# Query and key kept once as high and low parts, and four experts' scores made as pairs of 64-row products

## The chip, the cores and the metric

The kernel runs on one core of one Trainium2 chip. The metric is device microseconds of one execution; less is better. The profile names the engines PE (TensorE, the matrix unit, with PEld for its weight loads), DVE (VectorE), ACT (ScalarE), POOL (GpSimd) and SP (SyncE, which issues most DMAs).

## The reference, cut to what matters

Three blocks run one behind the other on 4 sequences (batches) of 576 rows: an attention with banded and strided masks, a gated feed-forward block, and a mixture of four dense attention experts. The change is in the last:

```
for e in range(E):                       # E = 4, Hd = 64, x is 4 x 576 x 512
    q = x @ wq[e];  k = x @ wk[e];  v = x @ wv[e]
    scores = scale * (q @ k.transpose(0, 2, 1))
    scores = np.where(causal, -1000000000.0, scores)
    scores = scores - scores.max(-1, keepdims=True)
    a = np.exp(scores)
    a /= a.sum(-1, keepdims=True) + 1e-09
    ye = a @ v @ wo[e]
    out += (weight of expert e in its row's top 2, else 0) * ye
```

The weights `wq` and `wk` are scaled by 200, so the scores are large and have to be made with nearly full fp32 precision.

## The kernel before, in words

**Units and order.** The work is cut into some 900 named units. `PLAN` lists them by rank; a name begins with its batch: `0k01` is a key projection of batch 0, `0s20` the scores of its query tile 2 for expert 0, `0p20` the transposes of those, `0a10` a value product, `0o12` an output projection. While the kernel is built, a `Recorder` collects every engine instruction of every unit with an estimated price (`price`), and `order` (line 384) gives them out one at a time: of the operations that could start about now on an engine it takes the one of least rank, where a change of TensorE's tile shape (`change`, with the constants `INTO` and `FROM`) sets an operation back by `stay` ranks. The order of each engine's instructions is then fixed as given out. All instructions are issued from one helper line, so every row of the profile says L484; tiles are told apart by name.

**Stages.** From the start to about 327 us the masked attention and the feed-forward block of all four batches run. Then a new SBUF pool (`p3`) is opened, and the dense experts of the four batches run until the end, with the projections of a later batch between the attention of an earlier one.

**Precision.** Products of the later blocks use the type fp32r, in which one operand is a rounded value. A value is split in a high part (rounded copy) and a low part (value minus copy); a product is then high x high, high x low and low x high (`split`, line 564). In the first block, and for batch 0 partly in the second, plain fp32 products are used; one such product in the program is two instructions in the trace.

**Queries and keys of the experts (`proj_units`, line 1356; `qkp`, line 1401).** A projection makes two experts' queries (or keys) at once, 64 rows each, in one PSUM bank. Queries: the bank is copied, both halves, for each of the two experts into a tile `Q` of 128 rows by 4 x 576; then, of each expert's columns, the 64 rows that aren't its own are overwritten with its low part. So a column block of `Q` holds high and low part of one expert one above the other. Keys: the bank is copied for both experts into `KH`, the low part into `KL`, and four DMAs from the POOL queue copy each expert's own rows into the other 64 rows. So each of `KH` and `KL` holds one expert's key part twice, one above the other.

**Scores (`tile_units`, `sc`, line 1505).** For a query tile t of 128 rows and an expert, two 128-row products with (t+1) x 128 columns are summed in one PSUM bank: `Q` with `KH`, and `Q` with `KL`. VectorE adds the mask, scales and takes the row extreme (tile `pe`), ScalarE makes the exponentials with their sum. The last 64 query rows of a sequence (`tail_units`, line 1550) are done for two experts side by side with a padded query tile `QT`, in four products of 288 columns per part.

**Banks.** Eight PSUM banks: three for scores (`ps_sc`), three for projections, value products and outputs (`ps_mm`), two for transposes (`ps_tr`).

Of the kernel before, what the change touches and what calls it, by code (L numbers as in the profile page):

```python
# [27 lines left out]
1S3 0P15 0Am5 0Am1 0W16 0Am6 1S4 0W18 0Am7 0P7 0P6 0L17 0W17 0P18 0Zg1 0Av4 2L1 0Av0 0P19 2L2 0Zg0 0Zk0 0P16 0Zg3 0P5 0P17
1V4 0P9 0Av6 0Zk2 1S6 0Av2 0Zk3 0P4 0Zk1 0Zm0 0Zg2 0sig 0P10 0Zm2 1T6 0Zm1 2z 1V6 0Zm3 0Av7 2L3 0Av3 1S8 1T8 1Ar0 0Av1 0P11
0P8 0Zm6 wl2 1Ar1 0Zm4 1V8 1Ak0 1Ak1 3z 0P3 1Ar2 3L0 0Zv4 0Zm7 0P1 0Zm5 0Zv0 1Ar3 1Ak3 0P2 0Zv1 0P0 0Av5 0x0 1Ag1 wl0 ws00  # L30
2S1 2S0 1Ak2 0Zv2 0Zv3 1Zr0 1Am4 1Zr1 1Zr2 2V1 1Zr3 1Ag0 1Am0 1Am1 1Zk0 2S4 2S3 1Ag2 0Zv6 2V4 2Ar0 2S6 2T6 1Am5 1Ag3 1Am2
1Am3 1Am6 1Am7 1Zg0 ws01 1Av4 1Zg1 wl1 0Zv5 1Zg2 2Ak0 1Zk2 3L1 2Ar1 2V6 2Ar2 0Zv7 1Zk1 1Av2 1Zg3 1Av3 3L2 1Zk3 1Av6 1Zm0 1Zm1
1Zm4 1Av0 1Av1 1Zm5 1Zm6 1Zm2 2S8 1Zm3 1Zv6 1Zm7 1Zv7 2T8 1Zv0 1Av7 2V8 2Ar3 2Ak3 2Ag1 3S1 2Ag3 2Ag0 3S0 3V1 2Ak2 ws10 3S3
3S4 2Ak1 2Am0 ws20 2Zr0 2Zr2 1Zv2 1Zv3 3V4 2Zk0 1Zv1 2Am2 1Av5 3S6 2Am3 1Zv4 1Zv5 ws21 2Zr1 2Ag2 2Am4 2Am1 2Am5 3L3 2Am6 2Am7
2Av6 2Zr3 2Zg2 3T6 3S8 2Av4 2Zg0 3V6 2Zg1 2Zg3 3T8 3V8 3Ar0 2Zk1 2Av5 2Zk2 2Zk3 3Ak0 2Zm2 2Zm6 2Zm3 2Av2 2Av0 2Av3 2Av1 2Zm0
2Zm1 2Zm4 3Ar1 2Zm5 2Zv2 3Ar2 3Ar3 0x1 3Ag0 2Zm7 2Zv3 3Zr0 2Zv6 3Ak2 3Ag2 3Ak1 2Zv4 1x0 2Av7 2Zv5 3Ag3 3Ak3 3Am4 0v0 3Am0
ws31 2Zv0 2Zv1 3Am1 3Ag1 3Zr2 3Zr1 3Am2 3Zk0 3Am5 3Am3 3Am6 3Am7 3Zr3 3Zg2 3Zg0 3Zg1 2u 2Zv7 3Zg3 3Av4 3Zk3 3Zk2 3Zk1 3Zm0
3Zm1 3Av6 3Av0 3Zm6 3Av2 3Zm2 3Zm3 3Zm4 3Zm5 3Zm7 3Zv4 3Zv6 3Zv0 3Av1 3Zv2 ws11 0k01 0k00 0q10 0k10 0q01 0k11 1u 0v4 0q00 0v1
0v2 0v3 0u 0g 3Av3 0q11 3Zv1 0s20 0s30 0s33 0s23 1k00 0t 1v1 1x1 3Zv5 0s21 1k01 0s31 0s22 0s00 1q00 0s32 0m2 0p22 0s01 0p20
0m3 0p31 1k10 3Zv3 0s02 1k11 0p33 0s40 0s03 0p30 0s10 3Zv7 0s12 1v0 0p23 0p32 1q11 1q01 2x0 0m0 0p21 0s41 0m4 3Av7 0p40 1q10  # L40
0p41 1s30 0s11 1v3 1v2 0s13 1n 1g 0m1 0p11 0p13 0p10 0p02 0p12 1s32 0p00 2q01 0a10 1s20 1s22 1s21 0a11 1s31 1s33 1m3 1p31
0p03 1p30 1s00 1s02 1s03 2x1 2q10 2k00 1s01 1s23 1m2 1s10 1s11 1s13 0p01 2k01 1s12 2k10 0o12 2q11 2t 1p21 0a00 0a01 0o01 0o11
2k11 2v3 1t 1s40 1m1 1p10 1s41 1p12 3Av5 3x1 2s30 2s33 1p32 2s32 2s20 2s21 1m0 1p02 1p22 2s23 2s22 2v2 2v4 3n 2s31 1p23 2q00
1p00 2v1 1p20 3k11 0o10 1p33 1m4 1p41 2s00 2s10 1p13 0o02 2s01 2s02 0o03 0o13 2v0 3k10 0o00 2g 2s03 2m0 1p40 3q10 1p01 1p11
# [1715 lines left out]
```

## Time and profile before

| what | us |
|---|---|
| time, median of 3 runs (lowest, highest) | 507.53 (507.33, 509.13) |
| the profiled execution's own time | 507.9 |
| its span (first to last instruction) | 506.1 |
| PE busy, weight loads busy | 495.5 (98%), 466.3 (92%) |
| DVE busy, ACT busy, POOL busy | 362.0, 288.9, 38.8 |

The span is what the trace shows; the rest of an execution's time, 1.8 us here, lies around it. Busy times of one engine are the union of its instructions. Matmuls overlap each other in the trace, so the pace of PE is read from the distance between the starts of neighbouring instructions, not from their durations.

### The profile page before, as it was taken

To read this page: it belongs to the slowest core of one execution; us is meant where nothing else is said; L and a number is where in the kernel's file an instruction comes from. 1 tells how busy PE (TensorE), PEld (TensorE's weight loads), DVE (VectorE), ACT (ScalarE), POOL (GpSimd) and SP (SyncE) were. 2 spreads that over 40 slices of the span, in tenths; PEclk is the share of its full clock that TensorE was granted. 3 is DMA by queue.
4 is the path that set the end of the run, shared out by engine and by line. 5 is a ranking of instruction groups with operands and counts; after the bars stand their busy time and mean duration, and the time that the engine had idled before them with its cause. 6 is when DMAs were issued, how large, how long until landed. Compare 5 with 4: busy or idle time off the path is not lost.

```text
span 506.1 us, 13080 instructions
## 1 busy us (share of the span) xinstructions
PE 495.5 (98%) x5080; PEld 466.3 (92%) x5080; DVE 362.0 (72%) x1230; ACT 288.9 (57%) x813; POOL 38.8 (8%) x95
## 2 busy tenths in 40 slices
PE   8799999999999999998999999999999999999997
PEld 7567799999999999998999999999998999899886
DVE  5899999894869563867574604258999887897941
ACT  6899976555548443535432533145676666367663
POOL 0000000000000000000000000053500411400000
PEclk9799999999999999999999999999999999999999
DMA  7998332332233122012321001164511422310122
GB/s 262 322 397 249 116 119 69 88 97 76 85 87 101 33 82 83 23 44 68 94 89 65 2 16 37 43 163 100 121 53 54 104 68 75 69 38 25 49 95 95
DMA packets 42008, 48.82 MB, mean 96 GB/s; under 512 B 14122, under 2 KB 36442, under 8 KB 41946
## 3 DMA queue, kind: packets, MB, share of 16 engines
q1 hardware_dynamic: 36826, 43.26, 27.2%
q0 software_dynamic: 5120, 4.72, 4.7%
q8 instruction: 40, 0.66, 0.6%
q14 instruction: 22, 0.18, 0.1%
HBM read 33.67 MB, written 9.44 MB: 85 GB/s over the span
## 4 chain that ended last, share of the span: by engine, by line
PE 92%; DMA 5%; DVE 2%; SPq 1%; issue 0%; ACT 0%; ACTq 0%
PE pk L484 19%; PE pv L484 19%; PE pr L484 11%; PE s L484 6%; PE pvv L484 5%; PE pw L484 5%; PE pq_True L484 5%; PE pq_False L484 5%; PE py L484 4%; PE pt L484 4%; DMA qkv<-in_strd_dram 2%; PE ss L484 2%; PE pol L484 2%; PE sl L484 2%; PE pos L484 2%; DMA qkv<-in_loc_dram 1%
## 5 line engine op out<-in xcount | busy, mean ns | idle before, releaser
L484 PE MATMUL pv<-kk,wvh 128*128 128x320 f32 (+1 forms) x512 | 103.8, 296 | 0.1
L484 PEld LDWEIGHTS pv<-kk,wvh 128*128 128x128 f32 x512 | 81.7, 188 | 0.8 <-DVE kk L484 0.3
L484 PE MATMUL pk<-xh,wkh 128*128 128x256 f32 (+1 forms) x224 | 65.7, 293 | 1.3 <-DVE sg L484 1.3
L484 PE MATMUL pk<-xl,wkh 128*128 128x256 f32 (+1 forms) x224 | 65.3, 291 | 0.0
L484 ACT ACTIVATE rf<-pk 128x320 f32<-128x320 f32 (+1 forms) x64 | 26.2, 409 | 48.5 <-PE pk L484 44.0
L484 ACT ACTIVATE pe<-pe,nm 128x384 f32<-128x384 f32 (+4 forms) x72 | 41.6, 580 | 10.2 <-DVE pe L484 6.7
L484 PEld LDWEIGHTS pk<-xh,wkh 128*128 128x128 f32 x224 | 42.0, 188 | 1.6 <-DVE sg L484 1.5
L484 PEld LDWEIGHTS pk<-xl,wkh 128*128 128x128 f32 x224 | 42.0, 188 | 0.0
L484 DVE TENSOR_TENSOR sg<-pv,sg 128x320 f32<-128x320 f32 (+1 forms) x32 | 14.4, 452 | 37.5 <-PE pv L484 37.2
L484 DVE CUSTOM_DVE_ANT_0 pe<-s,mcau 128x384 f32<-128x384 f32 (+4 forms) x72 | 32.8, 482 | 5.5 <-PE pt L484 3.1
L484 DVE TENSOR_TENSOR kk<-rf,kk 128x320 fp32r<-128x320 f32 (+1 forms) x64 | 28.5, 453 | 2.3 <-ACT kk L484 1.4
L484 PE MATMUL pt<-ident,pe 128*128 128x128 f32 x200 | 29.2, 272 | 0.0
L484 ACT ACTIVATE rf<-rf 128x320 f32<-128x320 f32 (+1 forms) x64 | 28.2, 444 | 1.6
L484 PE MATMUL pr<-xh,wrh 128*128 128x320 f32 (+1 forms) x96 | 28.4, 296 | 0.0
L484 ACT ACTIVATE el<-el,nm 128x64 f32<-128x64 f32 (+1 forms) x72 | 24.7, 344 | 6.3 <-DVE nm L484 5.8
L484 PE MATMUL pr<-xl,wrh 128*128 128x320 f32 (+1 forms) x96 | 28.2, 294 | 0.0
L484 ACT COPY sg<-pr 128x320 f32<-128x320 f32 (+1 forms) x30 | 11.8, 398 | 28.3 <-PE pr L484 28.3
L484 DVE CAST kk<-rf 128x256 fp32r<-128x256 f32 (+1 forms) x43 | 13.1, 305 | 18.8 <-ACT rf L484 15.8
L484 DVE SCALAR_TENSOR_TENSOR xf<-xd,mu,xT 128x256 f32<-128x256 f32 (+1 forms) x52 | 26.0, 509 | 0.5
L484 DVE TENSOR_SCALAR pe<-pe,sm 128x384 f32<-128x384 f32 (+4 forms) x72 | 25.4, 397 | 0.1
L484 ACT COPY aT<-pt 128x512 f32<-128x512 f32 (+3 forms) x55 | 22.5, 432 | 4.5 <-PE pt L484 3.6
L484 PEld LDWEIGHTS pt<-ident,pe 128*128 128x128 f32 x200 | 23.6, 140 | 0.9
(307 smaller groups left out, 1504.9 us busy)
## 6 DMA issues: line engine op xcount, KB each, us to landing
qkv<-in_strd_dram SPq DMA_DIRECT2D x8, 576.0 KB
wraw<-in_w_k_dram SPq DMA_DIRECT2D x8, 512.0 KB
wraw<-in_w_v_dram SPq DMA_DIRECT2D x8, 512.0 KB
qkv<-in_loc_dram SPq DMA_DIRECT2D x6, 592.0 KB
x_spill<-sg SPq DMA_DIRECT2D x16, 160.0 KB
x2f<-x_spill SPq DMA_DIRECT2D x4, 640.0 KB
out_dram<-ot SPq DMA_DIRECT2D x16, 160.0 KB
wraw<-in_w_r_dram SPq DMA_DIRECT2D x4, 512.0 KB
```

What stands on the lines that cost most here:

```text
L484: f[o.engine](*[now(x) for x in a], **{n: now(x) for n, x in k.items()})
```

## The change

Queries and keys are each kept once, as a high and a low tile in which two experts lie one above the other, as the projection makes them. The score of an expert is three 64-row products (high x high, low x high, high x low); products of two experts use the upper and the lower 64 rows of TensorE and write different banks. One unit now makes the scores of a query tile for all four experts, with three `ps_sc` banks and one `ps_mm` bank. The POOL DMAs, the second copies and the product of the two low parts are gone. The tail has three products per part in place of four, with `QT` padded at other places. Three constants of the planner change, a price for the new products is added, and `PLAN` is another list throughout.

```diff
@@ -21,32 +21,30 @@
 EL, ES = 3, 1
 PLAN = """
-wl3 0L1q 0L0q 0S3 0i 0L2q 0L1v 0S4 0L3q 0T3 0z 0V3 0L0 1L1 0T4 0V4 0S0 0S1 0L1 0T1 0S6 0S7 0L0v 0V1 0L3v 0W1 0T0 0L2 1z 0V0
-0Ar0 0W0 0Ar1 0T6 0T7 0L2v 0V6 0S9 0T9 0L1m 0S5 0W2 ws30 0L18 1L0 0S8 0V7 0L0m 0Ar2 0V9 0L5 0L6 0W6 0Ak0 0L4 0Ak1 0L3 0T5 0T8
-0L10 0V8 0S2 0Ar3 0L7 0L14 0W3 0L9 0W4 mc 0T2 0L11 0V2 0W5 0W7 0W11 0Ag0 0Ak3 0W14 0W9 1L2 0L8 0Ak2 0W10 0L19 0W8 0L12 1S1
...
-1o11 1o00 1o13 2a00 2a01 3s12 3s11 2a10 2a11 2o00 3p31 2o11 3m1 3p11 3p10 2o01 2o10 3p22 3p32 3p13 3p03 2o12 2o02 3p02 3p00
-2o13 2o03 3a10 3a11 3a00 3p12 3a01 3o10 3o12 3o01 3o03 3o00 3o13 3o11 3o02
+wl3 0L1q wl2 0L0q 0S3 0i 0T3 0z 0L2q 0L2v 0S4 0T4 0S0 0T0 0L1v 0L3q 0S1 0T1 0L1 0W1 0S6 0S7 0L0 0V4 0V3 0L0v 0V0 0L1m 0L3
+0L0m 0V1 0Ar0 0Ar1 0T7 0L5 0W0 0S9 0S5 0L8 0S8 1L1 0L3v 0L2 0W2 0T6 0V6 1L0 0Ak0 0Ak1 0L6 0W6 0V7 0Ar2 0W3 0T9 0S2 0Ag0 0Ag1
+0W5 0V9 0L7 wl0 0T8 0T5 0V8 0Ar3 0T2 0W7 0L4 0L12 0L9 1S1 0Ak2 ws30 0V5 0W4 1L2 1z 0V2 0Zr0 0L15 0L10 0W10 0L14 0W12 0W8 0L11
...
+3m3 3p33 3p32 3p21 3p30 3s1 3p41 3p40 2o13 3m1 3p13 3m0 2o02 3p01 3p00 3p02 3p11 3p31 3p20 2o12 3p12 2o11 2o00 2o03 2o01 2o10
+3a10 3a11 3p03 3p10 3a00 3a01 3o13 3o10 3o00 3o01 3o11 3o12 3o02 3o03
 """
@@ -190,7 +188,7 @@
     ENGINES = ("tensor", "vector", "scalar", "gpsimd", "sync")
     PORT = dict(vector="gpsimd", gpsimd="vector")
     NEAR = 0.10
-    INTO, FROM = 0.09, 0.14
+    INTO, FROM = 0.09, 0.20
     STAY = 15
     HOLD = 0.115
     WARM, FILL, IDLE = 80.0, 0.8, 0.35
@@ -314,10 +312,12 @@
                 return max(n, 32) / 2300, 0.38, ("f", 64, 32)
             if m == "transpose":
                 return (0.093 if rows < 110 else 0.109), 0.35, ("t", rows, cols)
+            if w.dtype == F32R and rows <= 64:
+                return max(n / 4460 + 0.003, 0.056), 0.35, ("f", False, True, "r")
             if w.dtype == F32R:
                 return max(n / 2230 + 0.003, 0.111), 0.35, ("r",)
             if rows <= 64 and n < 64:
-                return 0.028, 0.38, ("f", False, False)
+                return 0.036, 0.38, ("f", False, False)
             if cols == 128:
                 return n / 600, 0.38, ("w",)
             return n / 1200 + (0.006 if n < 100 else 0.020), 0.38, ("f", rows > 64, cols > 64)
@@ -1354,20 +1354,19 @@
     pst = {}
 
     def proj_units(b):
-        Qf = p3.tile([P, E * S], F32R, tag="Q", name=f"Q{b}")
-        Q = Qf.rearrange("p (e s) -> p e s", e=E)
-
-        QT = p3.tile([P, EP, 3, TW], F32R, tag="QT", name=f"QT{b}")
+        Q = [p3.tile([P, EP, S], F32R, tag=f"Q{x}", name=f"Q{x}{b}") for x in "hl"]
+        K = [p3.tile([P, EP, S], F32R, tag=f"K{x}", name=f"K{x}{b}") for x in "hl"]
+        QT = [p3.tile([P, EP, 2, TW], F32R, tag=f"QT{x}", name=f"QT{x}{b}") for x in "hl"]
         gwt = p3.tile([P, EP], F32, tag="gwt", name=f"gwt{b}")
-        KH = p3.tile([P, E, S], F32R, tag="KH", name=f"KH{b}")
-        KL = p3.tile([P, E, S], F32R, tag="KL", name=f"KL{b}")
         V = p3.tile([P, NT, GV], F32, tag="V", name=f"V{b}")
         gw = p3.tile([P, NT, E], F32, tag="gw", name=f"gw{b}")
-        pst[b] = dict(Q=Qf, QT=QT, KH=KH, KL=KL, V=V, gw=gw, gwt=gwt)
+        pst[b] = dict(Q=Q, QT=QT, K=K, V=V, gw=gw, gwt=gwt)
         leads = b % 2 == 0
 
         def zeros():
-            nc.gpsimd.memset(QT[:, :, 1, :].bitcast(F32), 0.0)
+            for x in QT:
+                for j in range(2):
+                    nc.gpsimd.memset(x[D * j:D * j + D, :, 1 - j, :].bitcast(F32), 0.0)
             nc.gpsimd.memset(V[TW:P, NT - 1, :], 0.0)
 
         nc.unit(f"{b}u", zeros)
@@ -1409,26 +1408,15 @@
                         nc.tensor.matmul(pm[:, :N], wh[:, kc, es], xl[:, kc, :N], start=False, stop=False)
                         nc.tensor.matmul(pm[:, :N], wl[:, kc, es], xh[:, kc, :N], start=False, stop=(kc == NKC - 1))
                     cs = slice(s0, s0 + N)
-                    es = slice(2 * ep, 2 * ep + 2)
-                    both = pm[:, :N].unsqueeze(1).to_broadcast([P, 2, N])
-                    H = KH if is_k else Q
-                    nc.copy(H[:, es, cs], both)
-                    if is_k:
-                        nc.vector.tensor_tensor(KL[:, es, cs], both, KH[:, es, cs].bitcast(F32), op=ALU.subtract)
+                    H, L = K if is_k else Q
+                    split(pm[:, :N], H[:, ep, cs], L[:, ep, cs])
+                return f
+
+            def tails():
+                for x, y in zip(QT, Q):
                     for j in range(2):
-                        e = 2 * ep + j
                         own = slice(D * j, D * j + D)
-                        oth = slice(D - D * j, 2 * D - D * j)
-                        if not is_k:
-                            nc.vector.tensor_tensor(Q[oth, e, cs], pm[own, :N], Q[own, e, cs].bitcast(F32), op=ALU.subtract)
-                            continue
-                        for K in (KH, KL):
-                            nc.gpsimd.dma_start(K[oth, e, cs], K[own, 2 * ep + 1 - j, cs])
-                return f
-
-            def tails():
-                for j in range(2):
-                    nc.vector.tensor_copy(QT[:, :, 2 * j, :], Q[:, j::2, TQ:].bitcast(F32))
+                        nc.vector.tensor_copy(x[own, :, j, :], y[own, :, TQ:].bitcast(F32))
 
             for ep in range(EP):
                 for is_k in (True, False):
@@ -1485,7 +1473,7 @@
 
     def attn_units(b):
 
-        Q, QT, KH, KL, V, gw, gwt = (pst[b][n] for n in ("Q", "QT", "KH", "KL", "V", "gw", "gwt"))
+        Q, QT, K, V, gw, gwt = (pst[b][n] for n in ("Q", "QT", "K", "V", "gw", "gwt"))
         for ci, (s0, N) in reversed(list(enumerate(CHUNKS))):
             cst = {}
             tiles = list(range(s0 // P, (s0 + N + P - 1) // P))
@@ -1502,24 +1490,25 @@
                 nk = (t + 1) * P
                 st = {}
 
-                def sc(e):
-                    def f():
-                        if e == 0:
-                            st["nm"] = p3.tile([P, 2 * E], F32, tag="nm3", name=f"nm3_{b}_{t}")
-                            st["sm"] = p3.tile([P, E], F32, tag="sm3", name=f"sm3_{b}_{t}")
-                        pe = p3.tile([P, nk], F32, tag=f"pe{t}", name=f"pe{b}_{t}_{e}", bufs=4)
-                        st["p", e] = pe
-                        qs = Q[:, e * S + t * P:e * S + t * P + P]
-                        nm, sm = st["nm"][:, e:e + 1], st["sm"]
-                        pm = ps_sc(f"s3_{b}_{t}_{e}")
-                        nc.tensor.matmul(pm[:, :nk], qs, KH[:, e, :nk], start=True, stop=False)
-                        nc.tensor.matmul(pm[:, :nk], qs, KL[:, e, :nk], start=False, stop=True)
+                def sc():
+                    nm = p3.tile([P, 2 * E], F32, tag="nm3", name=f"nm3_{b}_{t}")
+                    sm = st["sm"] = p3.tile([P, E], F32, tag="sm3", name=f"sm3_{b}_{t}")
+                    pm = [(ps_mm if e == E - 1 else ps_sc)(f"s3_{b}_{t}_{e}") for e in range(E)]
+                    for ep in range(EP):
+                        for i, (x, y) in enumerate(((0, 0), (1, 0), (0, 1))):
+                            for j in range(2):
+                                own = slice(D * j, D * j + D)
+                                nc.tensor.matmul(
+                                    pm[2 * ep + j][:, :nk], Q[x][own, ep, t * P:t * P + P], K[y][own, ep, :nk],
+                                    start=(i == 0), stop=(i == 2),
+                                )
+                    for e in range(E):
+                        pe = st["p", e] = p3.tile([P, nk], F32, tag=f"pe{t}", name=f"pe{b}_{t}_{e}", bufs=4)
                         nc.vector.tensor_tensor_reduce(
-                            out=pe, in0=pm[:, :nk], in1=mcau[:, 512 - nk:],
-                            scale=-0.125, scalar=BIG, op0=ALU.add, op1=ALU.min, accum_out=nm,
+                            out=pe, in0=pm[e][:, :nk], in1=mcau[:, 512 - nk:],
+                            scale=-0.125, scalar=BIG, op0=ALU.add, op1=ALU.min, accum_out=nm[:, e:e + 1],
                         )
-                        nc.scalar.activation(pe, pe, AF.Exp, bias=nm, scale=-1.0, accum_out=sm[:, e:e + 1])
-                    return f
+                        nc.scalar.activation(pe, pe, AF.Exp, bias=nm[:, e:e + 1], scale=-1.0, accum_out=sm[:, e:e + 1])
 
                 def norm():
                     sm = st["sm"]
@@ -1543,8 +1532,8 @@
                     return f
 
                 nc.unit(f"{b}m{t}", norm)
+                nc.unit(f"{b}s{t}", sc)
                 for e in range(E):
-                    nc.unit(f"{b}s{t}{e}", sc(e))
                     nc.unit(f"{b}p{t}{e}", trp(e))
 
             def tail_units(s0=s0, probs=probs):
@@ -1563,13 +1552,11 @@
                         nm, sm = st["nm"], st["sm"]
                         for i, (c0, n) in enumerate(TPARTS):
                             pm = ps_sc(f"s3_{b}_{t}_{ep}_{i}")
-                            for j in range(2):
-                                qs = QT[:, ep, j:j + 2, :].rearrange("p a s -> p (a s)")
-                                for h, K in enumerate((KH, KL)):
-                                    nc.tensor.matmul(
-                                        pm[:, :n], qs, K[:, 2 * ep + j, c0:c0 + n],
-                                        start=(j + h == 0), stop=(j + h == 2),
-                                    )
+                            for k, (x, y) in enumerate(((0, 0), (1, 0), (0, 1))):
+                                nc.tensor.matmul(
+                                    pm[:, :n], QT[x][:, ep].rearrange("p a s -> p (a s)"), K[y][:, ep, c0:c0 + n],
+                                    start=(k == 0), stop=(k == 2),
+                                )
                             last = nm[:, 2 * ep + i:2 * ep + i + 1]
                             nc.vector.tensor_tensor_reduce(
                                 out=pe[:, c0:c0 + n], in0=pm[:, :n], in1=mtail if i else mcau[:, :n],
```

## Rows read from the trace of the kernel before

**Rows 1.** The page: busy times, and granted clock in 40 slices of the span.
```profile
PE 495.5 (98%) x5080; PEld 466.3 (92%) x5080; DVE 362.0 (72%) x1230; ACT 288.9 (57%) x813; POOL 38.8 (8%) x95
PEclk9799999999999999999999999999999999999999
```

**Rows 2.** Windows: length, busy us (and instructions) by engine, clock, DMA share, GB/s.
```profile
0.00:12.60 12.60, 10.36 (x114) 9.17 (x114) 6.59 (x53) 7.60 (x32) 0.31 (x5) 1.00 0.79 261
12.60:25.00 12.40, 8.97 (x90) 7.08 (x92) 10.49 (x58) 11.09 (x48) 0.00 (x0) 0.72 0.91 323
...
200.00:250.00 50.00, 48.62 (x489) 47.77 (x489) 36.32 (x90) 24.70 (x59) 0.20 (x1) 1.00 0.19 55
...
345.00:380.00 35.00, 35.00 (x265) 33.66 (x266) 32.95 (x114) 24.74 (x63) 8.90 (x19) 1.00 0.36 88
```

**Rows 3.** Timeline of PE: start us, us, what; score products of 512, 384, 128 columns.
```profile
349.48 0.40 PE L484 MATMUL s<-KL,Q 128*128 128x512 f32 x1
349.71 0.34 PE L484 MATMUL s<-KH,Q 128*128 128x384 f32 x1
349.89 0.34 PE L484 MATMUL s<-KL,Q 128*128 128x384 f32 x1
...
352.67 0.22 PE L484 MATMUL s<-KH,Q 128*128 128x128 f32 x1
352.73 0.27 PE L484 MATMUL s<-KL,Q 128*128 128x128 f32 x1
352.84 0.34 PE L484 MATMUL pq_False<-x2h,wqh 128*128 128x256 f32 x1
```

**Rows 4.** Timeline of PE: transposes, 256-column scores, then 64-column tiles (py) begin.
```profile
438.63 0.38 PE L484 MATMUL pt<-ident,pe 128*128 128x128 f32 x2
438.77 0.36 PE L484 MATMUL s<-KH,Q 128*128 128x256 f32 x1
438.97 0.28 PE L484 MATMUL s<-KL,Q 128*128 128x256 f32 x1
439.09 0.28 PE L484 MATMUL s<-KH,Q 128*128 128x256 f32 x1
439.20 0.28 PE L484 MATMUL s<-KL,Q 128*128 128x256 f32 x1
439.41 0.49 PE L484 MATMUL py<-aT,V 128*64 128x320 f32 x2
```

**Rows 5.** Timeline of PE: such tiles end, full ones follow; products of the tail.
```profile
399.38 0.28 PE L484 MATMUL py<-aT,V 128*64 128x128 f32 x2
399.59 0.40 PE L484 MATMUL s<-KH,QT 128*128 128x288 f32 x1
399.82 0.30 PE L484 MATMUL s<-KL,QT 128*128 128x288 f32 x1
399.96 0.29 PE L484 MATMUL s<-KH,QT 128*128 128x288 f32 x1
```

**Rows 6.** Timeline of PE: 64-row fp32 products on two row halves; full fp32 products.
```profile
13.26 0.82 PE L484 MATMUL ss<-qkv 64*108 64x108 f32 x12 [0.73 <-DMA qkv<-in_strd_dram]
14.01 0.31 PE L484 MATMUL ptl<-ident,el 128*96 128x128 f32 x1
...
49.87 0.70 PE L484 MATMUL pk<-xw,w('k', 3, 1)_629 128*128 128x320 f32 x2
50.41 0.43 PE L484 MATMUL pk<-xw,w('k', 0, 0)_563 128*128 128x320 f32 x1
```

**Rows 7.** Groups from 327 us on: busy us, mean ns, idle before.
```profile
L484 DVE CUSTOM_DVE_ANT_0 pe<-s,mcau 128x384 f32<-128x384 f32 (+4 forms) x72 | 32.8, 482 | 5.5 <-PE pt L484 3.1 <-ACT pe L484 0.9 <-PE s L484 0.9
L484 DVE TENSOR_TENSOR Q<-pq_False,Q 64x320 fp32r<-64x320 f32 (+1 forms) x32 | 14.6, 456 | 3.1 <-ACT Q L484 2.4
L484 DVE TENSOR_TENSOR KL<-pq_True,KH 128x512 fp32r<-128x512 f32 (+1 forms) x16 | 12.1, 755 | 3.2 <-ACT KH L484 3.0
L484 DVE TENSOR_TENSOR yl<-py,yh 128x320 fp32r<-128x320 f32 (+1 forms) x16 | 7.2, 454 | 4.6 <-ACT yh L484 4.4
```

More of the change, by code (lines that the diff above doesn't have):

```diff
@@ L28 @@
[L28 to L44, printed above, removed]
@@ new lines @@
+1S6 1T6 0Av6 1V6 0Zg3 0P18 0P19 0P6 0Zk3 0Age 1S8 1T8 0Av2 2L1 0Zk2 0Zm2 1Ar0 1Ar2 1V8 0P11 0Zm3 0P10 0sig 0Av3 0Av4 0Av5
+0Zm0 0Av1 0P9 0P3 0P2 2S1 2S0 1Ak0 0P8 0Zm6 0P1 0Zm7 0Zm4 1Ar3 2V1 0Zm1 0Zv0 1Ar1 2S6 2S4 0P0 1Ag1 2S3 0Av7 1Ag3 0Zm5 2V4
+0Zv2 1Ak1 1Ak2 1Zr0 1Zr3 1Ag2 1Zk0 1Ak3 1Ag0 1u 0Zv6 1Am4 1Zr2 1Am6 1Am7 1Zr1 1Zk1 2T6 2L3 0Zv4 1Am2 1Am3 1Am0 1Am1 1Av4 1Zk2
+3z 1Am5 0Zv5 0Zv3 1Zg1 0x0 3L1 0Zv1 1Zg0 1Zg2 1Zk3 1Zm2 2Ar0 2Ar1 1Av2 ws31 0Zv7 1Zg3 1Av5 2V6 1Av0 1Av6 ws21 1Zm0 2S8 1Zm6
+2T8 2V8 1Zm1 3L0 1Zm3 2Ak0 2Ar2 1Av1 1Zv6 2Ar3 2Ag2 3S1 2Ak2 2Ak3 1Zm4 1Zm5 3S0 1Av3 1Zv0 3V1 1Zm7 2Ag1 1Zv7 3S3 3S4 2Ak1
@@ new lines @@
+2Am2 1Av7 3L2 2Ag3 2Zr0 1Zv4 wl1 ws11 3L3 1Zv1 1Zv2 1Zv3 2Ag0 2Am4 2Am3 2Am6 2Zr1 2Am5 2Am0 1Zv5 0x1 2Zr3 2Zr2 2Zg1 2Zg0 ws00
+2Zk0 2Zk2 2Am1 3Ar0 mc 3V4 3S6 2Zg2 2Zg3 2Am7 1x0 3T6 3V6 2Av4 3S8 2Av6 2Av7 3Ak0 3T8 3V8 1x1 2Av2 3Ar1 2Av3 2Zk1 3Ar2 2Av0
+0u 2Av5 2Zk3 2Av1 3Ar3 2Zm0 2Zm1 3Ag0 ws10 2Zm4 3Ak2 3Ak3 3Zr0 2Zm2 2Zm3 3Ag3 2Zm6 2Zm7 2Zv2 3Ag2 3Ak1 3Zr3 2Zm5 2Zv3 2Zv4
+3Ag1 2Zv6 3Am2 2Zv0 2Zv1 3Zk0 3Am3 2Zv5 3Zr2 3Zr1 3Zk1 3Zg1 3Am0 3Zk3 3Am1 3Am6 2Zv7 3Am4 3Am5 3Am7 3Zg2 3Av0 3Av4 3Zg0 3Zg3
@@ new lines @@
+3Av2 3Zk2 3Zm2 3Zm3 3Av6 3Zm6 0v1 3Zm7 3Zm0 3Zm1 3Zm4 3Zm5 3Zv4 3Zv6 3Zv0 3Zv2 0k00 0v0 0k10 ws01 0k11 0k01 0q11 0q01 0q00
+3Av7 0q10 0s1 0v2 0v4 1k01 0v3 1v0 0g 0s2 0m2 0m1 0p11 3Av5 1q00 1q10 0p20 3Zv1 0p10 0p21 2u 1q11 0s3 0m3 0p30 1q01 3Av1 0p22
+0s0 1v1 0t 0p32 0s40 0s41 0m0 1k00 2x0 0p13 0p02 1k11 0p03 1k10 0p23 0p00 1v2 3Zv3 3Av3 2k01 1v3 0p01 1s2 0m4 0p33 1t 0p41
+0p31 2k00 0p12 3Zv7 3Zv5 2x1 3u 2q10 0p40 2q11 1s1 1n 1g 0a00 0a10 0a11 0a01 1m1 1s0 1m0 1m2 0o10 0o12 1s40 1s41 2k10 0o03
+3x0 0o11 1s3 1m3 1p32 2v3 2v1 1p31 1p20 2t 1p22 1p10 1p00 2s40 1p01 0o01 0o02 2k11 1p12 1p13 1p21 2s41 2v0 1m4 1p41 0o00 1p02
@@ new lines @@
+2q01 1p30 1p40 1p03 0o13 2q00 2s2 2v4 3n 1p23 1p11 3x1 2v2 2g 3k01 1p33 3k00 2s3 2m3 2p32 2p30 2p33 1a10 1a11 1a00 1a01 2s1
+2m1 3q10 3v3 2m2 2s0 1o13 3v2 3k10 2m0 2p00 2p12 2p03 2p02 2m4 3k11 2p01 2p22 3q11 3t 2p13 2p10 1o03 3s3 3v1 1o11 1o02 2p40
+3s2 3v0 3g 1o00 1o10 2p21 2p20 2p31 3q01 3s40 3q00 1o12 2p23 3m2 2p41 3s41 1o01 3s0 3m4 2a10 2p11 2a00 2a11 2a01 3p23 3p22
+3m3 3p33 3p32 3p21 3p30 3s1 3p41 3p40 2o13 3m1 3p13 3m0 2o02 3p01 3p00 3p02 3p11 3p31 3p20 2o12 3p12 2o11 2o00 2o03 2o01 2o10
@@ L1503, in tile_units @@
                 st = {}
-                def sc(e):
-                    def f():
-                        if e == 0:
-                            st["nm"] = p3.tile([P, 2 * E], F32, tag="nm3", name=f"nm3_{b}_{t}")
-                            st["sm"] = p3.tile([P, E], F32, tag="sm3", name=f"sm3_{b}_{t}")
-                        pe = p3.tile([P, nk], F32, tag=f"pe{t}", name=f"pe{b}_{t}_{e}", bufs=4)
-                        st["p", e] = pe
-                        qs = Q[:, e * S + t * P:e * S + t * P + P]
-                        nm, sm = st["nm"][:, e:e + 1], st["sm"]
-                        pm = ps_sc(f"s3_{b}_{t}_{e}")
-                        nc.tensor.matmul(pm[:, :nk], qs, KH[:, e, :nk], start=True, stop=False)
-                        nc.tensor.matmul(pm[:, :nk], qs, KL[:, e, :nk], start=False, stop=True)
+                def sc():
[4 more added lines that the diff above has]
+                        for i, (x, y) in enumerate(((0, 0), (1, 0), (0, 1))):
+                            for j in range(2):
+                                own = slice(D * j, D * j + D)
+                                nc.tensor.matmul(
[4 more added lines that the diff above has]
+                        pe = st["p", e] = p3.tile([P, nk], F32, tag=f"pe{t}", name=f"pe{b}_{t}_{e}", bufs=4)
@@ L1565, in f @@
                             pm = ps_sc(f"s3_{b}_{t}_{ep}_{i}")
-                            for j in range(2):
-                                qs = QT[:, ep, j:j + 2, :].rearrange("p a s -> p (a s)")
-                                for h, K in enumerate((KH, KL)):
-                                    nc.tensor.matmul(
-                                        pm[:, :n], qs, K[:, 2 * ep + j, c0:c0 + n],
-                                        start=(j + h == 0), stop=(j + h == 2),
-                                    )
+                            for k, (x, y) in enumerate(((0, 0), (1, 0), (0, 1))):
[3 more added lines that the diff above has]
+                                )
                             last = nm[:, 2 * ep + i:2 * ep + i + 1]
```

7 lines of the change are left out of this document (2 added, 5 removed).

## The prediction, made before the change was run

> **What bounds the kernel now.** The page first: PE is busy for 98% of the span and its weight loads for 92%, while DVE stands at 72% and ACT at 57% [rows 1]. The reader is to see that only work on PE can shorten this kernel, as long as PE has something to do. The windows say where it has not: PE is idle for 2.2 us of the first 12.6 us, for 3.4 of the next 12.4 (where the granted clock averages 0.72, so part of it runs at the lower of the two levels), and for 1.4 between 200 and 250 us [rows 2]. In the stage of the change, from 327 us until the last product, PE is idle nowhere; the window shown stands for all of that stage. DVE is near its limit there too: 33.0 of 35 us from 345 to 380 us [rows 2]. So the change is worth what it takes from PE's queue, if DVE, ACT and the banks do not make PE wait; the distance between the starts of neighbouring products gives the price of each.
>
> **The products of the score tiles.** There are 4 batches x 4 experts x 2 products of each width, 32 of each. Start to start, a product of 512 columns takes 0.23 us, of 384 columns 0.18, two of 128 columns together 0.17, so 0.085 each [rows 3], and one of 256 columns 0.12 [rows 4]. Before: 32 x (0.23 + 0.18 + 0.12 + 0.085) = 19.7 us. After, there are 4 batches x 2 expert pairs x 3 = 24 pairs of products of each width. If two products of a pair run side by side, a pair takes what one full product takes; for 128 columns I take 0.11 and not 0.085, the longer of the two distances seen, since six different weight loads follow each other. After: 24 x (0.23 + 0.18 + 0.12 + 0.11) = 15.4 us. This saves 4.3 us.
>
> Does a pair run side by side? The trace has no fp32r product of 64 rows, but it has plain fp32 ones that write two banks from two row halves. Twelve of 108 columns start at 13.26 us and what follows starts at 14.01: 0.75 us [rows 6]. A full fp32 product costs 0.27 us per 320 columns (two in 0.54 us from 49.87 to 50.41) [rows 6], so 0.091 for 108; twelve in a row would take 1.09 us, six pairs 0.55. The measured 0.75 is six pairs and the change of tile shape costed below. So both products and weight loads of the two halves overlap, and I take full overlap. The other bound is none at all: 48 x 0.64 = 30.7 us.
>
> A rule of the Trainium skill speaks against the saving. By "TensorE: Matmul & The Clock Gate", section "LDWEIGHTS (loading the stationary operand)", a load's time follows its columns and not its rows, some 107 ns for 128 columns at 1.2 GHz; the 0.11 us of the narrow products agrees with it. By that rule 64 rows make no load shorter, and twelve loads that queued up would set the pace of every width below 512 columns. The rows of the fp32 pairs say that loads of two halves need not queue.
>
> **The tail.** 64 products of 288 columns become 48; each takes 0.14 us [rows 5]. This saves 16 x 0.14 = 2.2 us.
>
> **What the new shape costs.** A unit of 64-row products lies between full 128-row ones. The price of such a change is seen at the value products (`py`, 64-column tiles). Entry: the last score product of 256 columns starts at 439.20 and `py` at 439.41, 0.21 instead of 0.12 us: 0.09 more [rows 4]. Exit: the last pair of `py`, 128 columns, starts at 399.38 and needs, as fp32 side by side, 128/320 x 0.27 = 0.11 us; the next product starts at 399.59, so 0.10 us are lost, and its successor comes 0.23 us later in place of 0.14, so another 0.09 [rows 5]. Together 0.28 to 0.30 us. For 64-row tiles the 0.75 - 0.55 = 0.20 us above bears out the exit [rows 6]. There are 16 units, one per batch and query tile. Two of them can't follow each other at once, for each takes all three score banks. So 16 x 0.30 = 4.8 us are added. Bounds: where transposes follow, the second part of the exit is about half as large, and a unit beside `py` shares a change, 3.5 us at the least; 16 x 0.35 = 5.6 at most.
>
> In words of the Trainium skill ("TensorEngine Tiling (Array Packing)", "Key Properties"), a change of the tiling mode drains TensorE. It gives no time; the gaps above are what the trace has of it.
>
> **A smaller term.** A full product behind transposes pays 0.08 us once: 438.77 to 438.97 is 0.20 us, the next distance 0.12 [rows 4]. Of such places the timeline of before has 18, of which this is one: 1.5 us. With fewer, bundled units part of this goes; part goes to whatever follows the transposes then. Between 0 and 1.5, I take 0.7.
>
> **Other engines.** DVE loses the 14.6 us of low queries and the 12.1 us of low keys; 32 subtractions of one copy come in, at the price of the like `yl` (0.454 us) 14.5 us [rows 7]. So DVE is 12 us lighter, less some 2 us for twice as many copies into `QT`. ACT's copies become half as wide; 64 DMAs on POOL's queue and what waits for them go, and 12 more small clears of `QT` come to POOL. All of it I cost at nothing, neither way, because PE is idle nowhere in this stage: its cover is the queue of projections and value products. The cover could go in the last batch, when no projections are left. The loads of weights, the spills and SP's queue lose and gain no transfer here; the order moves them.
>
> **The wait that is added.** A unit takes four banks at once, and its four reductions on DVE come to 4 x 0.48 = 1.9 us on average [rows 7]. In PE's strict order, everything behind the unit waits until the four banks are free. The planner knows the banks and can put a unit late enough, and DVE gets lighter, so I take 0; the upper bound is a rival.
>
> **The new order.** It cannot fill what is full. What it can win is the idle time at the start, 2.2 + 3.4 + 1.4 us, and part of the slow clock there, at most 0.28 x 12.4 = 3.5 us: 10.5 us in all [rows 2]. DMA is busy at 0.79 and 0.91 in those windows, so the data's arrival limits this, and another order of loads can lose as easily. I take 0, between -5 and +3.
>
> **The sum.** -4.3 - 2.2 - 0.7 + 4.8 = -2.4 us. The profiled execution took 507.9 us, its span 506.1 and 1.8 around it; the sum makes it 505.5. It lies 0.4 above the median, so the median should go from 507.5 to 505.1. This is just at 0.5% (2.5 us), about what a measurement of this kernel tells from no change.
>
> **The rivals.** (a) The order also fills half of the start: 4 to 5 us more, 500.5 to 503. For it: the new list asks earlier for the values of batch 0's first strided pair; against it: DMA's load. 0.22. A start that is worse by as much as 4 us, 509: 0.06.
> (b) The banks: PE waits at the four-bank units for DVE's reductions. Place: the score units of batches 1 to 3, above all where the next tile's unit comes early. From 0.15 us per unit on the saving is eaten, from 0.30 the kernel is slower by more than 0.5%; at 0.45 it is 16 x 0.45 = 7.2 us, so 512. For it: DVE at 94% from 345 to 380 us; against it: DVE loses 10 us, and 16 units have 150 us to lie in. 0.15.
> (c) The weight loads of a pair queue. A pair then takes at least 2 x 0.11 us: 24 x (0.23 + 3 x 0.22) = 21.4 in place of 15.4 us, so 511. Against it: the 64-row rows. 0.06. It is what the skill's page on TensorE would give if loads could not overlap.
> (d) The pairs don't run side by side at all: 30.7 in place of 15.4 us, 520. 0.03.
>
> **How the numbers follow.** The forecast has 0.48; its own range is 503.5 to 507, and some two fifths of it lie below 505.0. Faster by over 0.5%: 0.20 from there and 0.22 from the order, 0.42. Within: the rest of the forecast, half of (b) and a part of the worse order, 0.40. Slower: half of (b), (c), (d) and the rest, 0.18. The range leaves out (c), (d), the far end of (b) and the best orders: 501.5 to 510.5.
>
> **What would show it.** Right: 64-row `s` products whose pairs start 0.23, 0.18, 0.12 and 0.11 us after each other; 48 tail products; gaps of 0.1 before and 0.2 us after each unit; no POOL DMA; PE idle only at the start. Wrong: PE idle before `s` or behind it, released by DVE; pairs at double distance; or a start whose full stretch begins some us earlier or later than 25 us.

## The result, and the profile after

The changed kernel takes 512.31 us, the kernel before beside it 507.54: a ratio of 1.0087 with a 95% interval of 1.0071 to 1.0103. Forecast were 505.1 us and a range of 501.5 to 510.5. The kernel became slower by 0.9%, and the time lies outside the range. Two of its 20 executions were slow, 966 and 1680 us; they are left out of the ratio, which is worked out from the single executions and need not be the quotient of the two medians.

The profiled execution has a span of 511.4 us, 5.3 more than before. Of the page, the busy times and the granted clock (40 slices), as in [rows 1], and the queues:

```profile
PE 496.0 (97%) x5128; PEld 461.1 (90%) x5128; DVE 348.9 (68%) x1217; ACT 283.3 (55%) x820; POOL 7.6 (1%) x43
PEclk9799999999999999999899999999999999999999
...
q1 hardware_dynamic: 36826, 43.26, 26.3%
q8 instruction: 40, 0.66, 0.5%
q14 instruction: 21, 0.17, 0.1%
```

DVE, ACT and POOL have less to do, and POOL's DMA queue is gone from the list. PE's busy time hardly moved, though the span grew: PE stood still for longer. One slice near the middle has a lower clock, which before no slice after the first two had.

The first thing to read is where the 5.3 us arise. The timeline gives a clean cut: the first projection of dense queries or keys (`pq`). It starts at 326.98 us before and at 334.88 after, 7.9 later; the last output product starts at 502.27 and 507.56. From the one to the other it is 175.3 us before and 172.7 after. So the stage that the edit is in won 2.6 us, and the blocks ahead of it, whose code did not change, lost 7.9.

Windows of the kernel after (length, busy us and instructions of PE, PEld, DVE, ACT, POOL, then clock, DMA share, GB/s):

```profile
75.00:125.00 50.00, 47.42 (x784) 45.34 (x783) 45.40 (x151) 30.50 (x97) 0.71 (x4) 1.00 0.36 104
...
200.00:250.00 50.00, 46.26 (x568) 45.00 (x567) 30.00 (x75) 22.19 (x51) 0.82 (x5) 0.99 0.16 50
245.50:248.50 3.00, 0.30 (x3) 0.10 (x1) 2.62 (x7) 1.45 (x6) 0.00 (x0) 1.00 0.00 0
249.20:252.60 3.40, 3.40 (x16) 3.40 (x15) 3.14 (x9) 2.98 (x8) 0.00 (x0) 0.50 0.53 183
...
334.90:507.50 172.60, 172.54 (x1445) 157.60 (x1444) 125.88 (x479) 98.08 (x283) 3.36 (x15) 1.00 0.17 53
```

and one window of the kernel before, whose row does not stand above:

```profile
75.00:125.00 50.00, 50.00 (x704) 49.13 (x703) 40.43 (x144) 28.56 (x84) 0.51 (x3) 1.00 0.31 89
```

In the first 25 us little changed: PE is busy for 19.6 us there, 19.3 before [rows 2], and the first product of the feed-forward block (`pk`) starts at 39.7 us, 39.5 before. Between 75 and 125 us PE now idles for 2.6 us, where it was full; DVE is busier there by 5 us and the DMA queues move 104 GB/s and not 89, and more of the attention of the next batches lies there: 160 of the small products `pol` and 100 of `ss` start in this window, before 80 and 50. Between 200 and 250 us PE idles for 3.7 us, 2.4 more than before [rows 2]. And from 249.2 to 252.6 us the granted clock is 0.50, the lower of the two levels, just behind an idle stretch of 2.75 us: half of 3.4, so 1.7 us of work are lost. Together 2.6 + 2.4 + 1.7 = 6.7 of the 7.9; the other 1.2 were not taken apart.

What PE waited for, from 25 to 330 us (us in total, times, longest):

```profile
PE pr L484 <- DVE sg L484: 2.7, 1, 2.7
PE pts L484 <- DVE es L484: 1.2, 2, 1.0
PE sl L484 <- DMA qkv<-in_loc_dram: 0.9, 1, 0.9
PE pk L484 <- ACT rf L484: 0.9, 1, 0.9
PE pv L484 <- DVE sg L484: 0.5, 1, 0.5
```

The longest is one wait, at 245.5 us. The chain of waits shows what stood behind it:

```profile
240.16 0.90 PE pos L484 x48
241.06 0.02 issue
241.07 4.44 DMA w3st<-in_wo_dram
...
245.88 0.43 DVE woh L484
...
248.10 0.41 DVE sg L484
248.51 0.04 issue
248.55 3.06 PE pr L484 x12
```

`w3st` is the staging tile for the dense weights, here those of `wo` (512 KB); `woh` and `wol` are their high and low part. The splitting instructions head the queues of ACT and DVE, and the rows of these two engines show both standing still for them; in brackets the idle time before:

```profile
245.81 0.62 ACT L484 CAST woh<-w3st 128x512 fp32r<-128x512 f32 x1 [6.94 <-PE pk L484]
...
245.88 0.43 DVE L484 CAST woh<-w3st 128x512 fp32r<-128x512 f32 x1 [5.19 <-PE pk L484]
...
248.01 0.49 DVE L484 TENSOR_TENSOR sg<-pv,sg 128x320 f32<-128x320 f32 x1
```

The profile names a product `pk`, which happened to end in the same moment, as what ended these two waits. The chain has it otherwise: the load lands at 245.51 us (241.07 + 4.44), and the splits start 0.3 us later. In e2 below, which has the same order here, the profile names the load itself for waits of 8.2 us of ACT and 6.4 of DVE.

Behind the splits wait the copies of the attention's result and the addition `sg<-pv`, which frees the bank that PE's next product, a `pr`, is to write. So a load whose result nobody needs for another 150 us stopped PE for 2.75 us. Before, the same load was issued ten us ahead of its splits, as the queue of SP and the view of the tile `w3st` show (of the second: nanoseconds, then first and last start):

```profile
221.95 0.35 SPq L484 DMA_DIRECT2D w3st<-in_wo_dram  x1
...
L484 DVE CAST woh<-w3st x1: 426/426/426, 231.7 to 231.7; 128x512 fp32r<-128x512 f32 x1
```

Why did it go out late? The chain says that the `pos` products released it, value products of an attention pair. The pools' addresses in the two built programs give the link. The pool of the dense weights is laid over that of the masked attention, and `w3st` lies in both kernels on the first of two buffers that take turns in holding a pair's queries, keys and values (`qkv`). Each pair takes the buffer that is free. Before, the last user of this first buffer is the last but one strided pair of batch 3 (unit 3V6), read for the last time at 221.8 us. In the new order the buffers fall out differently, and its last user is the very last pair (3V8), read until 241.0. The planner knows that one pool follows the other, but not which tile lies on which: in e5 and e6 below the addresses change and the order that it gives out stays.

### The profile page after: what moved, and what is told of

The parts are those of the page before. It is cut to its first block, busy times and chain, and to the rows that moved or that the text cites. A ratio compares the mean times of both kernels' runs of the same rounds, so it can differ in the third digit from the quotient of the medians.

```text
span 511.4 us, 13057 instructions
## 1 busy us (share of the span) xinstructions
PE 496.0 (97%) x5128; PEld 461.1 (90%) x5128; DVE 348.9 (68%) x1217; ACT 283.3 (55%) x820; POOL 7.6 (1%) x43
## 4 chain that ended last, share of the span: by engine, by line
PE 80%; DVE 10%; DMA 4%; ACT 4%; issue 1%; SPq 1%; DVEq 0%; ACTq 0%
PE pk L484 18%; PE pv L484 16%; PE pr L484 9%; PE pw L484 5%; PE pq_True L484 4%; PE pq_False L484 4%; PE pvv L484 4%; PE pt L484 4%; PE s L484 4%; PE py L484 3%; PE pol L484 2%; PE sl L484 2%; DMA qkv<-in_loc_dram 2%; DVE es L484 1%; ACT pe L484 1%; DMA qkv<-in_strd_dram 1%
## 5 line engine op out<-in xcount | busy, mean ns | idle before, releaser
L484 ACT ACTIVATE pe<-pe,nm 128x512 f32<-128x512 f32 (+4 forms) x72 | 41.5, 578 | 14.6 <-DVE nm L484 9.3
L484 DVE CAST kk<-rf 128x320 fp32r<-128x320 f32 (+1 forms) x42 | 13.1, 311 | 43.8 <-ACT rf L484 33.5
L484 DVE CUSTOM_DVE_ANT_0 pe<-s,mcau 128x512 f32<-128x512 f32 (+4 forms) x72 | 32.0, 482 | 4.1 <-PE pt L484 3.1
L484 ACT CAST xh<-xf 128x256 fp32r<-128x256 f32 (+1 forms) x30 | 12.9, 428 | 29.1 <-DVE xf L484 13.3
L484 ACT COPY aT<-pt 128x512 f32<-128x512 f32 (+3 forms) x56 | 24.3, 458 | 6.3 <-PE pt L484 5.8
```

Of the source, the lines that this page charges most:

```text
L484: f[o.engine](*[now(x) for x in a], **{n: now(x) for n, x in k.items()})
```

## The experiments

All kernels are the changed one or the one before, with one part exchanged; e7 is e1 with one thing more. The starts of the first feed-forward product (`pk`), of the first projection (`pq`) and of the last output product are read from each timeline; what lies between the last two is the dense stage. Two things have to be kept in mind. With a star, a value projection more (12 products `pvv`, 1.44 us) stands ahead of the first `pq` than in the other rows; beside those, take `pq` as 1.4 earlier and the dense stage as 1.4 longer. And the start itself differs between profiled executions: the first `pk` comes at 38.6 to 39.9 us with the old list and at 39.6 to 40.6 with the new one, in e7 at 43.2.

| run | time, us | kernel before beside it | ratio (95% interval) | first `pk` | first `pq` | dense stage |
|---|---|---|---|---|---|---|
| before | 507.54 | | | 39.54 | 326.98 | 175.3 |
| after | 512.31 | 507.54 | 1.0087 (1.0071 to 1.0103) | 39.74 | 334.88 | 172.7 |
| e1 old order ahead of the dense stage | 505.84 | 506.96 | 0.9978 (0.9959 to 0.9997) | 39.23 | 327.82* | 172.7* |
| e2 old score code, new order ahead | 520.74 | 506.96 | 1.0278 (1.0259 to 1.0297) | 40.17 | 338.78* | 176.6* |
| e3 load of `wo` planned later | 509.62 | 506.96 | 1.0050 (1.0031 to 1.0068) | 39.59 | 331.54 | 172.7 |
| e4 products not alternating | 513.55 | 506.96 | 1.0133 (1.0105 to 1.0161) | 39.85 | 335.86 | 172.8 |
| e5 staging tile moved | 508.72 | 507.79 | 1.0018 (0.9983 to 1.0053) | 40.57 | 330.95 | 172.5 |
| e6 before, staging tile moved | 512.43 | 507.79 | 1.0081 (1.0047 to 1.0115) | 39.93 | 331.87 | 175.0 |
| e7 a unit per pair | 514.00 | 507.79 | 1.0087 (1.0036 to 1.0138) | 43.22 | 331.64* | 177.2* |
| e8 new score code, old order | 509.97 | 507.79 | 1.0022 (0.9999 to 1.0046) | 38.58 | 325.55 | 178.4 |
| e9 old order up to 126 us | 507.34 | 507.04 | 1.0013 (0.9993 to 1.0033) | 38.60 | 327.86 | 172.7 |
| e10 e1 again | 506.19 | 507.04 | 0.9988 (0.9955 to 1.0021) | 39.33 | 328.08* | 172.7* |

**Is it the order, or the code? (e1, e2)** The list of ranks is cut at the dense stage.

```diff
 # e1: the changed kernel
-PLAN = new list; INTO, FROM = 0.09, 0.20; return 0.036, 0.38
+PLAN = first 389 names of the old list, then the rest as in the new one; INTO, FROM = 0.09, 0.14; return 0.028, 0.38
 # e2: the kernel before
-PLAN = old list; INTO, FROM = 0.09, 0.14; return 0.028, 0.38
+PLAN = first 388 names of the new list, then the rest as in the old one; INTO, FROM = 0.09, 0.20; return 0.036, 0.38
```

> The changed code, with the first 389 places of the old list (everything up to the first key projection of the experts) and the planner's two old constants, then the new list's order for the rest. Theory (the list's first part costs some 7 us in waits and slow clock before 327 us, the new score code saves some 2.5): the front goes back to before, and the saving is left: 507.5 - 2.5 = 505, between 504 and 506. Rival (the new score code itself costs time, by its banks or its changes of tile shape): 508 to 512.

> The opposite: the old score code, with the first 388 places of the new list and its constants, then the old order for the rest. Theory: the waits before 327 us come along without any of the change's code: 507.5 + 7 = 514.5, between 513 and 517. Rival (the code is to blame): 506.5 to 508.5.

With the old order ahead and the new code and order behind, the first `pq` starts 7.1 us earlier than in the changed kernel, 8.5 with the projection that stands ahead of it: the whole loss is back. The dense stage's 172.7 is the same number by accident. Like for like it is 174.1, 1.4 more than in the changed kernel; 1.0 of that are two waits at 379.8 and 381.1 us, where the joined order makes PE wait for DVE and ACT. With the new order ahead and the old code behind, the loss is there, and the time is larger than I expected by 6 us: the first `pq` starts 11.8 us late, 10.4 like for like, with a wait of 4.0 us at the place of the 2.75, and the dense stage has waits of its own, 2.0 us. Only the order of work, with the planner's constants that belong to it, is common to the two kernels with the late start; the score code is not.

**Is it the late load? (e3, e5, e6)** First the planner was told that loads into `w3st` land 8 us later, so that it places the splits later.

```diff
-                o.end = link + 0.5
+                o.end = link + (8.5 if any(t.kw["name"] == "w3st" for t in o.tiles) else 0.5)
```

> The changed kernel, but the planner is told that the four loads into the weights' staging tile land 8 us later than it thinks, so that VectorE's and ScalarE's splits of wo are ordered later; instructions are the same ones. Theory (that split, queued ahead of its data, holds up both engines' queues, and PE waits 2.7 us for it at 245 us and then runs 3.4 us at half clock, 1.7 lost): 4.4 us come back, 508, between 507 and 509.5. Rival (the stretch is short of ready work anyway, another wait takes its place): 511 to 513.

The wait of 2.75 us and the slow clock are gone, and 3.3 us are back; a wait of 0.8 us at 265.0 us is new, and one at 92 us grew from 0.2 to 0.7. The time lies 0.1 us above the expected range. But the planner moved other instructions too, so this alone does not prove the cause. The next pair changes addresses and nothing else: three other weight tiles are taken from the pool first, which pushes `w3st` onto the second buffer, and the tiles behind it, `woh` among them, along with it. The order of instructions on every engine stays.

```diff
+            if any(t.kw["name"] == "w3st" for t in o.tiles):
+                for t in self.first:
+                    t.real()
+                self.first = ()
             for f, a, k in o.calls:
...
+    nc.first = (wkkh, wkkl, wvgh)
```

> The changed kernel, same list, same program order on every engine; only the places in memory of the dense weights' tiles differ: the staging tile of wo lies under the buffer that holds unit 3V6's keys and values (last read at 227.4 to 228.3 us by the profile after) and no longer under the one that unit 3V8 reads last (240.1 to 241.0). Theory (the load of wo waits for that last reader, the splits stand at the head of ACT's and DVE's queues behind the load, and PE waits for DVE): the load goes out near 228.5 and lands near 233, the wait of 2.75 us at 245.5 goes, and with it the half clock at 249.2 to 252.6 (some 1.7 us): 507.9, between 507 and 509. Rival (the load is late for another reason, or another wait takes the place): no change, 512.

> The kernel before, with the same exchange of places: there it puts wo's staging tile under the buffer that unit 3V8 reads last (230.7 to 231.6 us), where it was free at 221.8. Theory: the load goes out at 231.6 in place of 221.95, lands near 236, and the splits that stand in ACT's and DVE's queues at 231.7 hold what is behind them for some 4 us; PE's wait at 233 grows from 1.3 us to 3 or 4: 510, between 509 and 512. Rival (PE has enough queued to pass over it): 507.5.

Both moved as the theory has it, e6 to 0.4 us above its range. In e5 PE's waits from 25 to 330 us are

```profile
PE pts L488 <- DVE es L488: 1.4, 2, 1.2
PE sl L488 <- DMA qkv<-in_loc_dram: 1.2, 1, 1.2
PE pk L488 <- ACT rf L488: 0.9, 1, 0.9
```

The one at 245 us is gone, the clock stays at 1.00, and `pq` starts 3.9 us sooner, though the first `pk` came 0.8 later. One step of the expectation was wrong: the load does not go out at 228.5 but at 237.76. It stands on SP's queue behind two spills that wait for the running sum `sg`:

```profile
234.03 3.64 SPq L488 DMA_DIRECT2D x_spill<-sg  x2
237.76 0.38 SPq L488 DMA_DIRECT2D w3st<-in_wo_dram  x1
```

3.3 us earlier than after were enough, since DVE then idled for only 0.31 us before its split, which the profile puts down to this load. In e6 the kernel before gets the fault. Queues of SP and DVE, and PE:

```profile
232.16 0.35 SPq L488 DMA_DIRECT2D w3st<-in_wo_dram  x1
...
235.86 0.43 DVE L488 CAST woh<-w3st 128x512 fp32r<-128x512 f32 x1 [4.55 <-issue]
...
238.65 0.58 PE L488 MATMUL pk<-xh,wkh 128*128 128x256 f32 x1 [5.04 <-DVE sg L488]
239.03 0.41 PE L488 MATMUL pk<-xl,wkh 128*128 128x256 f32 x1
239.24 0.41 PE L488 MATMUL pk<-xh,wl('k', 0, 0)_1225 128*128 128x256 f32 x1
```

The load goes out right behind the last read of the other buffer, DVE stands still, PE's wait of 1.3 us grows to 5.0, and the products behind it start 0.21 us apart in place of 0.12: the half clock comes back with the idle stretch (granted clock 0.64 on average from 238.6 to 243.0 us). The kernel before became 4.6 us slower by addresses alone. That the address of `w3st` is the one that counts, and not that of a tile moved along with it, rests on the waits: the splits start right behind the landing of its load.

**Where is the rest? (e9)** The old list up to 126 us, the new one from there. The turns of the two buffers then come out as before, so `w3st` lies on the early one.

```diff
-PLAN = new list
+PLAN = old list up to 1Ag3 (126 us), then the rest as in the new one
```

> The changed kernel with the old list up to the unit 1Ag3 (some 126 us) and the new list from there on, with the new planner figures. Two things differ from the changed kernel before 327 us: the stretch of 75 to 125 us is the old one, in which PE had no wait (there the new order lost 2.6 us to four waits), and wo's staging tile lies, as in the kernel before, under the buffer that unit 3V6 reads last. Theory (these two places hold nearly all of what the new order lost): 512.3 - 4.4 - 2.6 = 505.3, between 504.5 and 507. Rival (the new order loses as much elsewhere, or the splice makes new waits): 508 or more.

`pq` starts at 327.86 us: 7.0 of the 7.9 are back. But 1.1 of the 7.0 lie ahead of the first `pk`, which came early in this execution; from there to the first `pq` it is 295.1 us in the changed kernel, 289.3 here and 287.4 before. So the stretch of 75 to 125 us and the load of `wo` hold three quarters of the loss, 5.9 of 7.7. The two were not told apart by a run of their own; e5 gives what the load is worth. The profiled execution took 506.45; the median, 507.34, lies 0.3 above the range. One wait of 0.9 us is left between 200 and 330 us, at the attention's transposes, and two of together 0.7 us before 200.

**Do the pairs run side by side by themselves? (e4)** Here three products of one expert are queued, then the three of its partner.

```diff
-                        for i, (x, y) in enumerate(((0, 0), (1, 0), (0, 1))):
-                            for j in range(2):
+                        for j in range(2):
+                            for i, (x, y) in enumerate(((0, 0), (1, 0), (0, 1))):
```

> The changed kernel, with the three products of one expert behind each other and then those of the other, in place of alternating. Theory (two 64-row products overlap only as neighbours in PE's queue): of 12 products in a unit only three neighbouring pairs are on different row halves, 9 steps in place of 6: 16 units x 3 x 0.16 us = 7.7 us more, 520. Rival (PE picks from its queue, or the halves did not overlap before either): 512.

The dense stage kept its length, as the rival said. The time is of two executions, and 1.2 us above that of the changed kernel; 1.0 of it arises ahead of the first `pq` and was not taken apart. More on the products in the last section.

**What does a change of tile shape cost? (e7)**

```diff
 # e7: e1's kernel; in the list two units per tile in place of one
-                    for ep in range(EP):          # one unit: both pairs, four banks
+                for ep in range(EP):              # two units: a pair each, two banks
+                    nc.unit(f"{b}s{t}{ep}", sc(ep))
```

> Order of before up to the dense stage, that of the changed kernel behind it, as in the run at 505.84; but a score unit computes one pair of experts (one pair of products three times) in place of two pairs, so 32 units and not 16. By the prediction's term each change of shape costs 0.30 us: 16 more give 505.8 + 4.8 = 510.6, less where two units stand side by side; 509, between 507 and 511. Rival (the change of shape costs next to nothing, or smaller units let the softmax start sooner): 505 to 506.5.

The dense stage takes 177.2 us, 4.5 more than in e1, so 4.5 / 16 = 0.28 us for each of the 16 further units. e1 has 1.0 us of waits there and e7 none; without them it is 5.5 / 16 = 0.34. Another bank changed with it: all four score banks are now of `ps_sc`. The time, 514.00, lies 3 us above the expected range. In the profiled execution (514.46) the rest of the distance to e1 is not of the change: the start took some 4 us longer with the same order (last section). Of the other executions no trace is kept; they took from 509.74 to 514.52 us.

**Does the dense stage need its new order? (e8)**

```diff
-PLAN = new list; INTO, FROM = 0.09, 0.20; return 0.036, 0.38
+PLAN = old list, a tile's score unit where the last of its four stood; INTO, FROM = 0.09, 0.14; return 0.028, 0.38
```

> The changed score code in the whole old list, with the old planner figures; the unit of four experts stands where the last of the four units stood. If the order behind 327 us is worth nothing by itself, the code's 2.4 us show: 505 to 505.5. Rival (four scores in one unit, four banks at once and the exponentials of four experts behind each other, need the new order, and PE waits for banks or for probabilities): 508 to 511, with waits of pt or s on ACT in the dense stage.

The rival was right, but for the engine, DVE and not ACT: the dense stage takes 178.4 us, 3.1 more than with the old code, and PE waits there for DVE, for probabilities, transposes' banks and score banks:

```profile
PE pt L484 <- DVE pe L484: 1.1, 2, 0.6
PE pt L484 <- DVE aT L484: 0.6, 1, 0.6
PE s L484 <- DVE nm L484: 0.4, 1, 0.4
PE pvv L484 <- DVE nm L484: 0.4, 1, 0.4
```

That is 2.5 us of waits; the rest was not taken apart.

**The best version.** e1, run twice, gave ratios of 0.9978 and 0.9988 to the kernel before. The first interval ends just below 1, the second includes it: it is faster than the changed kernel by 1%, and against the kernel before at most by a few tenths of a per cent.

## Why the prediction was wrong

**The step that failed is the new order, "I take 0, between -5 and +3".** It was +7.9 us ahead of the dense stage. The argument was that the order "cannot fill what is full" and can win only at the start. It looked at the gain alone: the 300 us in which PE was full were taken as safe, but with another order they are not full (47.4 of 50 us from 75 to 125). The bound of +3 came from the start, by the load of the DMA queues there, and little moved at the start. 6.7 of the 7.9 us arose at 75 to 125 and at 236 to 253 us, in stretches that the prediction had taken as full or nearly so [rows 2]. I had asked what the new order could fill and not what slack each wait had: `wo`'s load had ten us to spare before. The diff of the list could not show the loss: the load's unit, `wl3`, stands first in both lists. What changed is who reads the memory under it last.

**"The loads of weights, the spills and SP's queue lose and gain no transfer here; the order moves them"** was true and stopped one step short. No transfer was added, but one was held for another reader of the same memory, and behind it stood two engines (e5, e6).

**The rivals.** None had this mechanism. The range's upper end came in part from the bank wait (b), which does not show in the changed kernel: from 334.9 to 507.5 us PE is idle for 0.06 us. It shows in e8, with the old order: 0.8 of the 2.5 us of waits there are for the reductions of a four-bank unit (`nm`). So part of the new order's work is to make room for these units. That the wait costs 0 was right with this order only, and so is the sum: the code by itself, in the old order, costs 3.1 us in the dense stage.

**The dense stage: -2.6 us measured, -2.4 forecast.** The agreement holds for the new order as a whole (after, e9); joined to the old one in e1 the stage gains 1.2 like for like. The start-to-start distances summed by kind say how the terms stood. The tail: 9.0 to 6.8 us, -2.2 as forecast. The score tiles with their changes of shape and the transposes' term were to give -4.3 + 4.8 - 0.7 = -0.2: the tile products went from 21.66 to 18.34, -3.3, and what stands behind them grew, transposes by 1.8, projections and value projections by 1.0, output products by 0.3, while the products with the values fell by 0.1, so -0.4. The pace of the pairs is as forecast, as PE's timeline shows (starts and durations in us) for 256, 512 and 128 columns:

```profile
349.09 0.30 PE L484 MATMUL pq_False<-x2h,wql 128*128 128x320 f32 x1
349.33 0.39 PE L484 MATMUL s<-Kh,Qh 64*128 64x256 f32 x2
349.56 0.28 PE L484 MATMUL s<-Kh,Ql 64*128 64x256 f32 x2
349.67 0.28 PE L484 MATMUL s<-Kl,Qh 64*128 64x256 f32 x2
...
350.03 0.28 PE L484 MATMUL s<-Kl,Qh 64*128 64x256 f32 x2
350.23 0.39 PE L484 MATMUL pvv<-wvgh,x2h 128*128 128x260 f32 x1
350.46 0.28 PE L484 MATMUL pvv<-wvgl,x2h 128*128 128x260 f32 x1
...
364.81 0.40 PE L484 MATMUL s<-Kh,Qh 64*128 64x512 f32 x2
365.04 0.40 PE L484 MATMUL s<-Kh,Ql 64*128 64x512 f32 x2
...
368.68 0.27 PE L484 MATMUL s<-Kh,Qh 64*128 64x128 f32 x2
368.79 0.28 PE L484 MATMUL s<-Kh,Ql 64*128 64x128 f32 x2
```

A pair takes 0.12, 0.23 and 0.11 us. The change of shape is seen in full between projections: 0.24 us instead of 0.15 into it, 0.23 instead of 0.12 for the first pair, 0.20 and 0.23 instead of 0.12 behind it, so 0.09 + 0.11 + 0.08 + 0.11 = 0.39 us. I had missed the first pair's 0.11; beside transposes it is less, and e7's mean of 0.28 to 0.34 bears out the 0.30.

Rival (c), queued weight loads, is out: two loads of 128 columns fit in the 0.11 us of the narrowest pair. The prediction took the 0.11 us of a narrow full product as the time of its load; the distance just before is 0.06 [rows 3], so that row did not show it. By the Trainium skill's "TensorE: Matmul & The Clock Gate", section "LDWEIGHTS (loading the stationary operand)", a load of 64 rows is as long as one of 128, and the trace agrees in its records, 186 ns on average for 64 rows and 189 for 128. But loads of two row halves overlap here.

## What to carry to other kernels

A stage in which an engine is full may be so by the order of the work alone. If a change replaces that order, forecast what each transfer and each wait has in reserve, not only which gaps could be filled; a list that is new throughout is a risk of several us by itself, larger here than the edit that it came with. Where one pool is laid over another, look up which tile lies on which and who reads the old one last: an early load of something needed late can then stop the engines that are to unpack it, and all that stands behind.
